# Two residuals moved down ScalarE's queue in an S5 and sparse-MLP kernel

## The chip, the cores and the metric

The kernel runs on one core of a Trainium2 chip. The metric is device time in microseconds (us), best read as the median of several executions. Each execution also has a span, which is the time from the core's first to its last instruction; it is 1.8 to 2.4 us shorter than the time (runs of before).

## The reference, cut to what matters

The input is 2048 tokens of 1024 values, and a core handles them in 16 chunks of 128 tokens.

```python
xn = _layernorm(x)
# A: diagonal state space model, a scan over all tokens
Bu = einsum("bld,pd->blp", xn, B_bar)
h  = Lam_bar * h + Bu[:, t]            # for each token t
yA = 2 * einsum("blp,dp->bld", hseq, Cmat).real + xn * Dskip
# B: the two tokens with the largest xn @ w_r go through a gated MLP;
#    its result is added to xn at those tokens
return x + yA + B(xn)
```

Each chunk thus needs the residual `x + xn`, which is `x * (1 + rstd) - mean * rstd`. This is ScalarE's `xa` (chunks 9 to 12 get theirs from VectorE), and it is added to the matmul result `pY` at the very end of the chunk's work. Chunks go in pairs: chunks 2f and 2f+1 share the matmuls into `pB` and the casts that empty it into `u` (`u` f/j is the j-th of the pair's eight). Other names in the traces: `sum`, `sq`, `rstd` and the negated mean `nmean` are the steps to a chunk's norm `xn`; `xnT` is its transpose, made by a DMA; `gb` is the cast of the scan's result `gf`, and `hT` is made from it for the output matmuls `pY`.

## The kernel before: the parts concerned

The program doesn't write its instructions in a fixed order. A planner in it simulates the engines at build time and emits one operation after another; the smaller `key` goes first among those that are ready. A table `ADJUST` shifts single keys. The emitted order is fixed: on the chip each engine works through its own queue.

```python
ADJUST = {
    ('x', 4): -5.4, ('x', 6): 45.2, ...
    ('Bh', 1, 0): -4.0,
}
...
def add(self, name, eng, dur, fn, deps=(), key=0.0, takes=(), mb=0.0, lag=0.0):
    key += self.adjust.get(name[0], 0.0) + self.adjust.get(name, 0.0)
...
def load_x(c):                      # x for the norm: four buffers
    xt_tiles[c] = xin.tile([128, D], BF16, name="xt")
    nc.sync.dma_start(out=xt_tiles[c][:], in_=x2[c * T:(c + 1) * T, :])
...
def ln_apply_act(c):                # the norm, on ScalarE for chunks 6 to 15 (L375)
    nc.scalar.activation(out=xn_tiles[c][:], in_=xt_tiles.pop(c)[:], func=ACT.Identity,
                         bias=nmr_all[:, c:c + 1], scale=rstd_all[:, c:c + 1])
...
def evac_u(f, j):                   # empties one of the three pB buffers (L653)
    nc.scalar.copy(out=u_tiles[f][:, :, j, :], in_=pB_tiles.pop((f, j))[:])
...
def load_xr(c):                     # x again, for the residual: ONE buffer (L807)
    xr = xrp.tile([128, D], BF16, name="xr")
    nc.sync.dma_start(out=xr[:], in_=x2[c * 128:(c + 1) * 128, :])
    y_tiles["xr", c] = xr

def residual(c):                    # L812
    xa = outp.tile([128, D], F32, name="xa", tag="xa", bufs=1)
    nc.scalar.activation(out=xa[:], in_=y_tiles.pop(("xr", c))[:], func=ACT.Identity,
                         bias=nmr_all[:, c:c + 1], scale=rstd1_all[:, c:c + 1])
...
add(("xa", c), "ACT", 1.13, lambda c=c: residual(c), [("xr", c), ("nmr", c), ("nmr1", c)],
    key=c - 25, takes=xa_take)
```

`xr` has one buffer, so chunk 4's reload can only be issued when residual 3 has been taken, and everything behind residual 4 on ScalarE waits when that reload is late.

## Time and profile before

| | before |
|---|---|
| time, first three runs | 266.67, 265.92, 267.57 us |
| profiled run | 267.47 us, span 265.2 us |
| busy in the span | TensorE 97%, VectorE 95%, ScalarE 60% |
| TensorE's waits from 60 us on | 1.4 us on a `u` cast, 0.4 us in the tail |
| ScalarE's idle time before residual 4 | 1.43 us |

In the profile PE is TensorE, DVE is VectorE, ACT is ScalarE, SPq is SyncE's queue, which issues most DMA transfers. L812 is line 812 of the program. A line of waits reads: engine, line, what it waited for, total us, times, longest. A line of a timeline reads: start, duration, engine, line, operation, output<-inputs, shapes, count, and in brackets the idle time before it and what ended it. The prediction below shows the lines on which it rests.

### The profile page before, as it was taken

The page shows a single profiled execution, that of the slowest core. Times are in us where ns is not written, and L with a number is a line of the kernel's source. Part 1 is how long each engine was busy: PE and PEld are TensorE (multiplying, and loading weights), DVE is VectorE, ACT ScalarE, POOL GpSimd, SP SyncE. Part 2 cuts the span into 40 slices and gives each one's busy share as a digit, 9 for nine tenths or more (in the row PEclk, how much of TensorE's full clock was granted, in tenths as well). Part 3 has the DMA queues.
Part 4 walks back from the last instruction along what each step waited for, and adds up shares of the span by engine and source line. Part 5 has one row for each costly group of instructions (what it writes and reads, how often), then busy time and mean ns, then how long its engine had stood idle before and what let it go on. Part 6 is the DMA issues. An engine that isn't in the chain of part 4 may idle for free.

```text
span 265.2 us, 5503 instructions
## 1 busy us (share of the span) xinstructions
PE 257.2 (97%) x2211; PEld 172.2 (65%) x2211; DVE 250.7 (95%) x329; ACT 159.1 (60%) x281; POOL 82.8 (31%) x126
## 2 busy tenths in 40 slices
PE   6999999999999999979999999999999999999994
PEld 6899888774688557445756586465763776644461
DVE  6999999999999999998979999999998999999992
ACT  3799999968799999796524347124551533145110
POOL 4220304473636430540140226205260409011020
PEclk9999999999999999999999999999999999999999
DMA  8999999996451127416212197588868884780311
GB/s 192 206 213 198 177 282 195 270 280 219 121 158 43 40 59 218 84 40 160 81 59 62 29 360 231 184 274 281 292 229 265 275 299 161 254 303 20 116 47 40
DMA packets 66165, 46.51 MB, mean 175 GB/s; under 512 B 45844, under 2 KB 52122, under 8 KB 66140
## 3 DMA queue, kind: packets, MB, share of 16 engines
q1 hardware_dynamic: 65788, 45.82, 62.9%
q8 instruction: 17, 0.28, 0.5%
q0 software_dynamic: 144, 0.27, 0.4%
q10 hardware_dynamic: 208, 0.07, 0.1%
q14 instruction: 8, 0.07, 0.1%
HBM read 30.94 MB, written 4.20 MB: 133 GB/s over the span
## 4 chain that ended last, share of the span: by engine, by line
PE 54%; DVE 27%; ACT 11%; issue 4%; DMA 3%; DVEq 0%; ACTq 0%
PE pB L647 26%; PE pY L851 22%; DVE gf L720 5%; PE pG L1045 3%; ACT xn L350 2%; DMA xr<-in_A_x_dram 2%; DVE ot L865 2%; DVE gb L713 2%; ACT xa L812 2%; DVE hT L761 2%; ACT xn L344 2%; DVE m L762 2%; DVE st L335 2%; ACT xn L375 1%; DVE v L699 1%
## 5 line engine op out<-in xcount | busy, mean ns | idle before, releaser
L851 PE MATMUL pY<-CT,hT 128*128 128x512 bf16 (+1 forms) x528 | 118.4, 373 | 0.4 <-DVE hT L763 0.4
L647 PE MATMUL pB<-xnT,BT 128*128 128x256 bf16 (+1 forms) x1088 | 117.3, 266 | 1.4 <-ACT u L653 1.4
L647 PEld LDWEIGHTS <-BT 128*128 128x128 bf16 x1088 | 99.4, 98 | 16.5 <-issue 4.7
L851 PEld LDWEIGHTS <-hT 128*128 128x128 bf16 x528 | 49.2, 98 | 52.6 <-issue 3.2
L736 POOL TENSOR_TENSOR cw<-gf,tL 128x16 f32<-128x16 f32 (+1 forms) x38 | 35.1, 926 | 138.3 <-DVE gf L720 137.4
L720 DVE TENSOR_TENSOR_SCAN gf<-R,v 128x1040 f32<-128x1040 f32 (+1 forms) x38 | 69.0, 1851 | 0.2
L653 ACT CAST u<-pB 128x512 bf16<-128x512 f32 x64 | 36.5, 580 | 34.7 <-PE pB L647 34.6
L726 ACT CAST gb<-gf 128x1024 bf16<-128x1024 f32 (+1 forms) x38 | 32.4, 863 | 22.9 <-DVE gf L720 22.8
L812 ACT ACTIVATE xa<-xr,nmr_all,rstd_all 128x1024 f32<-128x1024 bf16 x12 | 14.9, 1241 | 24.3 <-DMA xr<-in_A_x_dram 7.4
L761 DVE TENSOR_TENSOR hT<-gb,E2c 128x2048 bf16<-128x2048 bf16 (+2 forms) x22 | 20.4, 928 | 1.6 <-ACT gb L726 1.6
L701 DVE TENSOR_TENSOR v<-v,m 128x2048 bf16<-128x2048 bf16 (+2 forms) x22 | 20.6, 938 | 0.8
L763 DVE TENSOR_TENSOR hT<-hT,m 128x2048 bf16<-128x2048 bf16 (+2 forms) x22 | 20.5, 934 | 0.8
L699 DVE TENSOR_TENSOR v<-u,E1c 128x2048 bf16<-128x2048 bf16 (+2 forms) x22 | 20.4, 929 | 0.2
L700 DVE TENSOR_TENSOR m<-u,E1s 128x2048 bf16<-128x2048 bf16 (+2 forms) x22 | 20.5, 930 | 0.0
L762 DVE TENSOR_TENSOR m<-gb,E2s 128x2048 bf16<-128x2048 bf16 (+2 forms) x22 | 20.5, 930 | 0.0
L865 DVE TENSOR_TENSOR ot<-pY,xa 128x512 bf16<-128x512 f32 (+1 forms) x25 | 16.0, 656 | 3.1 <-PE pY L854 1.8
L751 POOL CAST v<-cy 128x16 bf16<-128x16 f32 (+1 forms) x19 | 14.1, 744 | 1.4
L350 ACT ACTIVATE xn<-xt,nmean_all 128x1024 bf16<-128x1024 bf16 x12 | 13.8, 1151 | 0.3
L744 POOL TENSOR_TENSOR cy<-cw 128x16 f32<-128x16 f32 (+1 forms) x19 | 12.8, 675 | 1.5
L344 ACT ACTIVATE xn<-xt 128x1024 bf16<-128x1024 bf16 x12 | 12.7, 1055 | 0.0
L375 ACT ACTIVATE xn<-xt,nmr_all,rstd_all 128x1024 bf16<-128x1024 bf16 x10 | 12.4, 1242 | 0.3
L752 POOL TENSOR_TENSOR v<-cy,v 128x16 bf16<-128x16 f32 (+1 forms) x19 | 10.3, 544 | 1.5
(148 smaller groups left out, 184.2 us busy)
## 6 DMA issues: line engine op xcount, KB each, us to landing
wt<-in_B_w_up_dram SPq DMA_DIRECT2D x14, 512.0 KB, 5.0
wt<-in_B_w_gate_dram SPq DMA_DIRECT2D x14, 512.0 KB, 4.3
wt<-in_B_w_down_dram SPq DMA_DIRECT2D x14, 512.0 KB, 3.7
xt<-in_A_x_dram SPq DMA_DIRECT2D x16, 256.0 KB, 3.4
xr<-in_A_x_dram SPq DMA_DIRECT2D x16, 256.0 KB, 2.5
out_dram<-ot SPq DMA_DIRECT2D x31, 128.0 KB, 2.2
Drow<-in_A_Dskip_dram SPq DMA_DIRECT2D x1, 256.0 KB
xnT<-xn SPq DMA_TRANSPOSE x10, 2.8
```

Of the source, the lines that this page charges most:

```text
L647: nc.tensor.matmul(out=pB[:, ri, ts_], lhsT=BT[ri][j][:, k, :], rhs=xnT_tiles[f][:, k, ts_], start=(k == 0), stop=(k == DT - 1))
L653: nc.scalar.copy(out=u_tiles[f][:, :, j, :], in_=pB_tiles.pop((f, j))[:])
L699: nc.vector.tensor_tensor(out=rot, in0=u, in1=both(E1c, js), op=ALU.mult)
L700: nc.vector.tensor_tensor(out=m[:, :, js, :], in0=u[:, ::-1], in1=E1s[:, :, js, :], op=ALU.mult)
L701: nc.vector.tensor_add(out=rot, in0=rot, in1=m[:, :, js, :])
L720: nc.vector.tensor_tensor_scan(out=flat(gf), data0=flat(R[:, js, :]), data1=flat(v[:, ri, js, :]), initial=0.0, op0=ALU.mult, op1=ALU.add)
L726: nc.scalar.copy(out=gb_tiles[c][:, ri, js, :], in_=gf_tiles[c, js.start, ri][:, :, 2:])
L736: nc.gpsimd.tensor_tensor(out=cw_tiles[c, js.start][:, ri, :, 0:n], in0=g.unsqueeze(1).to_broadcast([128, 2, n]), in1=tL[:, ri, :, js], op ...
L761: nc.vector.tensor_tensor(out=rot, in0=g, in1=E2c[:, :, js, :], op=ALU.mult)
L762: nc.vector.tensor_tensor(out=m[:, :, js, :], in0=g[:, ::-1], in1=both(E2s, js), op=ALU.mult)
L851: nc.tensor.matmul(out=pY[:], lhsT=h_tiles[c][:, ri, j, :], rhs=CT[ri][h][:, j, d0:d0 + w], start=first and c in SKIP_DVE and ri == rs[0] ...
L865: nc.vector.tensor_add(out=y_tiles["ot", c][:, d_], in0=y_tiles.pop(("pY", c, dh))[:], in1=y_tiles["xa", c][:, d_])
```

## The change

Its intent is to let ScalarE do urgent things first: residual 4 isn't needed until chunk 4's output is added, and it goes behind the norm of chunk 11; residual 6 goes back by one operation.

```diff
     ('gT', 1): 64.4,
     ('Bh', 1, 0): -4.0,
+    ('xa', 4): 35.0, ('xa', 6): 20.0,
 }
```

No instruction is added or taken away. On ScalarE residual 4 goes behind norm 11; residual 6 goes behind `u` 4/4. The added line shifts line numbers by one, so L812 is L813 in the changed kernel.

## The prediction

> **What bounds the kernel now.** The page's first part and its two waits tables for TensorE and VectorE come first.
>
> ```profile
> PE 257.2 (97%) x2211; PEld 172.2 (65%) x2211; DVE 250.7 (95%) x329; ACT 159.1 (60%) x281; POOL 82.8 (31%) x126
> ```
>
> TensorE and VectorE are both nearly full, ScalarE is at 60%. A change on ScalarE can therefore only pay where ScalarE holds one of the two full engines up. The waits of TensorE from 60 us to the end are just these:
>
> ```profile
> PE pB L647 <- ACT u L653: 1.4, 1, 1.4
> PE pY L851 <- DVE hT L763: 0.4, 1, 0.4
> ```
>
> There is a single wait of 1.4 us on ScalarE (a `u` cast that empties a `pB` buffer), and a 0.4 us one in the tail at 259 us. The chain of work that ended last, around the first, reads (start, duration, what):
>
> ```profile
> 101.57 1.14 ACT xa L812
> 102.71 0.03 ACT lv L314
> 102.73 5.39 DMA xr<-in_A_x_dram
> ...
> 108.20 1.25 ACT xa L812
> 109.45 0.09 ACT nmean_all L382
> 109.54 0.94 ACT gb L726
> ...
> 113.69 0.57 ACT u L653
> 114.27 0.04 issue
> 114.31 1.91 PE pB L647 x16
> ```
>
> So the end of the kernel hangs, at 102.7 us, on a reload of x into `xr`; then ScalarE runs without a gap from the residual (L812) to the `u` cast; then TensorE starts. After 114.31 the chain is TensorE without a wait to 231 us and mostly VectorE after that. The timeline of ScalarE gives the stretch in single operations:
>
> ```profile
> 106.59 0.19 ACT L344 ACTIVATION_READ_ACCUMULATOR xn<-xt 128x1 f32 x1
> 108.20 1.25 ACT L812 ACTIVATE xa<-xr,nmr_all,rstd_all 128x1024 f32<-128x1024 bf16 x1 [1.43 <-DMA xr<-in_A_x_dram]
> 109.36 0.19 ACT L382 ACTIVATE nmean_all<-sm 128x1 f32<-128x1 f32 x1
> 109.44 1.03 ACT L726 CAST gb<-gf 128x1024 bf16<-128x1024 f32 x1
> ...
> 112.55 1.24 ACT L375 ACTIVATE xn<-xt,nmr_all,rstd_all 128x1024 bf16<-128x1024 bf16 x1
> 113.69 0.56 ACT L653 CAST u<-pB 128x512 bf16<-128x512 f32 x1
> ```
>
> The trace shows no chunk numbers. I took them from the order in which the unchanged program's own planner emits ScalarE's work: sum 11, residual 4, negated mean 11, `gb` 5, square 11, rstd 11, norm 11, `u` 4/0, sum 10 and so on. The L812 at 108.20 is thus the residual of chunk 4, and the L375 at 112.55 the norm of chunk 11. VectorE suffers twice nearby, each time on a `gb` cast from ScalarE:
>
> ```profile
> 110.51 1.23 DVE L761 TENSOR_TENSOR hT<-gb,E2c 128x2048 bf16<-128x2048 bf16 x1 [0.42 <-ACT gb L726]
> ...
> 118.50 1.26 DVE L865 TENSOR_TENSOR ot<-pY,xa 128x512 bf16<-128x512 f32 x2
> 120.91 1.23 DVE L761 TENSOR_TENSOR hT<-gb,E2c 128x2048 bf16<-128x2048 bf16 x1 [1.15 <-ACT gb L726]
> ```
>
> The reader should see that the residual isn't urgent (its taker, the L865 of chunk 4, runs at 118.50, nine microseconds after it), and that it stands ahead of things that are.
>
> **What the Trainium skill says.** "PSUM — Partial Sum Buffer", section "Engine vs sequencer instructions": the queues of ScalarE, VectorE and GpSimd are strict FIFO, and matmuls complete in program order. The trace agrees: ScalarE idled 1.43 us before the residual, although the next operation needed only the sum that had ended at 106.78, and `gb` only a scan that VectorE had finished at 106.41. "ScalarE: Activation LUTs", section "What ACT_TABLE_LOAD costs": 186 ns, plus about 93 ns for each per-partition pointer operand, plus 0.833 ns an element, and neighbours overlap by about 93 ns. For 1024 elements with two pointers that is an estimate of 1225 ns; the trace has 1.24 us, and the next operation starts 1.14 to 1.16 us after the residual does. I use the trace's 1.15.
>
> **The change part by part.** Nothing is added or removed: same instructions, another order.
>
> First, residual 4. Without it, the negated mean follows the accumulator read at about 106.81 (0.03 us after its end, as elsewhere in this timeline) instead of 109.36. From there to the `u` cast ScalarE takes 113.69 - 109.36 = 4.33 us, with all its inputs there. So the place behind norm 11 is reached at 106.81 + 4.33 = 111.14. I read "behind the norm" as right behind it, ahead of `u` 4/0. The residual runs there with its data long landed (108.1), and `u` starts at 111.14 + 1.15 = 112.29 instead of 113.69: 1.40 us sooner. That is just the vanished idle time; the residual's own 1.15 us stays ahead of the `u` cast.
>
> TensorE: its matmul before the wait ends at 112.89, the wait is 1.42. The cast would now end at 112.29 + 0.56 = 112.85, so TensorE goes on at about 112.9. **Gain there: 1.4 us.** VectorE: `gb` comes 2.5 us sooner, so the 0.42 wait goes; the second `gb` (119.83, in ScalarE's unbroken run behind `u`) also comes 1.4 sooner, so most of the 1.15 wait goes too: 0.42 + about 1.0 = 1.4 us, no more and no less than TensorE's.
>
> A part may be lost at once. The `pY` ring has three buffers, so chunk 5's second output half (TensorE L844 at 119.93) needs the first L865 of chunk 4. That one ended at 118.50 + 0.68 = 119.18 and moves by only 0.42, to 118.76; TensorE would be there at 119.93 - 1.42 = 118.51. An estimated wait of 0.3 us, giving a net gain of 1.1 to 1.4.
>
> Second, residual 6. It runs at 127.10 after a wait of 3.26 us, and `u` 4/4 stands behind it, starting at 128.25. Letting that cast go first frees a `pB` buffer some 3 us sooner. But the trace shows no TensorE wait there: three `pB` buffers are in turn, and the taker of this one is the third of three matmul groups that start at 128.22 and take 1.75 us each, near 131.7. The taker of the residual itself comes at 135.40, after a wait on TensorE. **Worth 0**, perhaps a guard against a wait that residual 4's shift would have opened.
>
> Sum: 0 for the second, 1.1 to 1.4 us for the first. TensorE has no wait from 114 to 259 us, and what feeds it later (scans, casts, weight loads released by its own matmuls) starts from events that move along. I pass 1.2 us on to the end: 266.7 - 1.2 = 265.5 us, or 0.45%.
>
> **The rivals.** (a) The gain is eaten later: VectorE, at 95%, may hold the old pace. For it: in 150 to 250 us VectorE is idle less than 2 us. Against: its two waits at 110 and 120 go as well, and at 135.40 it waits 1.27 us for TensorE, so it is not the leader there. This would leave 266.2 to 266.7. (b) The late residual becomes a new wait: it frees the only `xr` buffer 2.8 us later (end about 112.3 instead of 109.4), so chunk 5's reload starts later. "DMA: Bandwidth & Descriptors", section "Anatomy of one DMA — SWDGE (gpsimd) path", says a semaphore wait sits on the issuing sequencer, before dispatch. If that reload stayed ahead of norm 11's transpose on SyncE, the transpose (now due 111.2 instead of 113.81) would wait to 112.3, still earlier than before. An unloaded `xr` takes 2.5 us to land here, so by 115 to 116; residual 5 needs it at about 119.4 (120.78 less 1.4). Its single `xa` buffer is free after the two L865 of chunk 4, at 119.76 less 0.42 = 119.34: in time by nothing, so some tenths may go astray. That would make 265.8 to 266.3. (c) More than the sum: if `u` 4/0 were put ahead of the residual, ScalarE would gain 2.5 us on it, but TensorE had only 1.42 to lose, and the rest would be VectorE's; 265.2 at best, not the 261.3 that 2% asks for.
>
> **Range and chances.** The three runs of before spread from 265.92 to 267.57, so a median may be off by about 0.5 us. With that on both sides of 265.5, and rival (a) on the upper side: 264.4 to 266.9. Two per cent is 5.3 us, and the waits that the change can touch sum to 1.4 us on TensorE. Slower by 2% needs a new wait of over 6 us, of which I found none. Faster 0.01, same 0.98, slower 0.01.
>
> **What would show it.** Right: the L812 of chunk 4 starts near 111.1 with no idle time before it; TensorE's 1.4 us wait on `u` is gone or under 0.3; VectorE's waits of 0.42 and 1.15 on `gb` shrink to some tenths together; a small TensorE wait on L865 may stand near 118.5; residual 6 has a `u` cast ahead of it and nothing else differs there; the span falls by about 1.2. Wrong: a new DMA wait of `xr` before residual 5, a transpose that starts later than 113.8, or TensorE waits after 120 us that give the gain back. The likeliest cause of a miss is that the planner also reorders DMA starts or another engine's work, which the change's title doesn't tell.

## The result, and the profile after

| | before | after |
|---|---|---|
| median, 6 runs each | 266.55 us | 266.14 us |
| lowest to highest | 265.92 to 267.57 us | 265.91 to 266.31 us |
| ratio of the fast runs | | 0.998, 95% interval 0.996 to 1.0001 |
| profiled span | 265.2 us | 264.0 us |

A ratio in this document is the mean time of one kernel's fast runs over that of the other's of the same rounds, so it isn't quite the ratio of the medians quoted. The result is "same" at 2%. The interval just includes 1, so these six runs alone don't show a gain clear of noise; all jobs together do (see "Why the prediction was right or wrong"). The two profiles differ by 1.2 us, just what was predicted; the medians differ by 0.41 us, a third of it. And the lowest run is the same for both: what the change took away is the long runs.

The timeline of ScalarE in the changed kernel, to set against the one in the prediction:

```profile
106.58 0.19 ACT L345 ACTIVATION_READ_ACCUMULATOR xn<-xt 128x1 f32 x1
106.80 0.20 ACT L383 ACTIVATE nmean_all<-sm 128x1 f32<-128x1 f32 x1
106.91 1.03 ACT L727 CAST gb<-gf 128x1024 bf16<-128x1024 f32 x1
...
110.00 1.24 ACT L376 ACTIVATE xn<-xt,nmr_all,rstd_all 128x1024 bf16<-128x1024 bf16 x1
111.15 0.56 ACT L654 CAST u<-pB 128x512 bf16<-128x512 f32 x1
111.62 1.24 ACT L813 ACTIVATE xa<-xr,nmr_all,rstd_all 128x1024 f32<-128x1024 bf16 x1
```

No idle time stands in brackets any more: the negated mean (L383) follows the accumulator read at once, the `u` cast starts 2.5 us sooner than before (113.69), and the residual finds its data there. TensorE's waits from 60 us on in the changed kernel:

```profile
PE pY L852 <- issue: 0.5, 3, 0.2
PE pY L852 <- DVE hT L764: 0.4, 1, 0.4
PE pY L845 <- DVE ot L866: 0.2, 1, 0.2
```

The 1.4 us on `u` is gone; a new one of 0.2 us on VectorE's L866 stands in its place. (The 0.5 us of "issue" is in profiles of the kernel before too, e1 for one.) VectorE's timeline has the two places where it waited for a `gb` cast:

```profile
110.00 1.22 DVE L762 TENSOR_TENSOR hT<-gb,E2c 128x2048 bf16<-128x2048 bf16 x1
...
119.48 1.23 DVE L762 TENSOR_TENSOR hT<-gb,E2c 128x2048 bf16<-128x2048 bf16 x1 [0.21 <-ACT gb L727]
```

Of 0.42 and 1.15 us only 0.21 is left; a new wait of 0.32 us on TensorE's `pR` has come in at 124.70. So the mechanism works in the profile as the sum had it. The question for the experiments is where two thirds of the gain went in the median.

### The profile page after: what moved, and what is told of

Read it like the earlier page. It is cut to its first block, busy times and chain, and to the rows that moved or that the text cites. A ratio compares the mean times of both kernels' runs of the same rounds, so it can differ in the third digit from the quotient of the medians.

```text
span 264.0 us, 5484 instructions
## 1 busy us (share of the span) xinstructions
PE 256.6 (97%) x2191; PEld 172.9 (66%) x2211; DVE 250.6 (95%) x329; ACT 159.1 (60%) x281; POOL 83.5 (32%) x126
## 4 chain that ended last, share of the span: by engine, by line
PE 52%; DVE 36%; DMA 3%; issue 3%; ACT 2%; SPq 2%; DVEq 0%
PE pB L648 26%; PE pY L852 20%; DVE gf L721 9%; DVE ot L866 3%; PE pG L1046 3%; DVE hT L762 3%; DVE m L763 3%; DMA CT<-in_A_C_im_dram 2%; DVE v L702 2%; DVE v L700 2%; DVE m L701 2%; SPq L288 2%; DVE gb L714 2%; DVE st L336 2%; DMA xt<-in_A_x_dram 1%
## 5 line engine op out<-in xcount | busy, mean ns | idle before, releaser
L852 PE MATMUL pY<-CT,hT 128*128 128x512 bf16 (+1 forms) x508 | 114.8, 372 | 1.7 <-issue 0.5
L813 ACT ACTIVATE xa<-xr,nmr_all,rstd_all 128x1024 f32<-128x1024 bf16 x12 | 14.9, 1238 | 20.2 <-DMA xr<-in_A_x_dram 6.0
L866 DVE TENSOR_TENSOR ot<-pY,xa 128x512 bf16<-128x512 f32 (+1 forms) x25 | 16.0, 656 | 3.1 <-PE pY L855 1.8
L753 POOL TENSOR_TENSOR v<-cy,v 128x16 bf16<-128x16 f32 (+1 forms) x19 | 11.1, 585 | 1.5
```

The costliest lines, as they stand in the source:

```text
L852: nc.tensor.matmul(out=pY[:], lhsT=h_tiles[c][:, ri, j, :], rhs=CT[ri][h][:, j, d0:d0 + w], start=first and c in SKIP_DVE and ri == rs[0] ...
L866: nc.vector.tensor_add(out=y_tiles["ot", c][:, d_], in0=y_tiles.pop(("pY", c, dh))[:], in1=y_tiles["xa", c][:, d_])
```

## The experiments

**Theory A**: residual 4's stall isn't the same in each run, because the landing of its `xr` load isn't; the one profiled run had a long one, and a run with no stall has nothing to gain. **Theory B**, the rival: the stall is 1.4 us in each run, and the missing part is lost elsewhere or is noise outside the span. Two further rivals are that residual 6 carries part of the effect, and that the order on ScalarE matters by itself, without the load. Where an edit would move line numbers, it was put on an existing line. All twelve runs gave correct results.

### The kernel before, beside itself

The program is unchanged.

> The kernel before, unchanged, run beside itself. Theory A (the gain is the stall of residual 4 on its xr load, and that stall differs from run to run, so the predicted 1.2 us was the stall of the one profiled run): this profile shows another idle time before the L812 of chunk 4 than 1.43 us, and the runs spread over more than 1 us. Theory B (the stall is the same 1.4 us in each run and the missing 0.8 us was lost elsewhere, or is noise outside the span): idle time again near 1.4 us and span near 265.2 us in each run.

The median was 266.73 us (266.48 to 267.17, 6 runs) against 266.41 us (265.8 to 267.49) of the 11 runs of before in the same job, ratio 1.0011, interval 0.9987 to 1.0035. Its profile has the stall at another size (ScalarE's timeline):

```profile
107.69 1.24 ACT L812 ACTIVATE xa<-xr,nmr_all,rstd_all 128x1024 f32<-128x1024 bf16 x1 [0.85 <-DMA xr<-in_A_x_dram]
```

TensorE's wait on `u` was 0.8 us in this run and its span 264.6 us. The spans of the job's 11 runs of before tell it better: six lie at 264.0 to 264.2 us, five at 265.0 to 265.4 us, none between. (The six own runs are less clean: 264.2, 264.3, 264.6, 265.0, 265.1 and 265.3 us.) The best half of before is already as short as the changed kernel. The spread of the times over the six own runs, 0.7 us, is under the 1 us that A expected; the 11 runs of before show 1.7 us.

### The changed kernel, and each half alone

```diff
-    ('Bh', 1, 0): -4.0,
+    ('Bh', 1, 0): -4.0, ('xa', 4): 35.0, ('xa', 6): 20.0,     # e2
+    ('Bh', 1, 0): -4.0, ('xa', 4): 35.0,                      # e3
+    ('Bh', 1, 0): -4.0, ('xa', 6): 20.0,                      # e4
```

> The changed kernel, with the two numbers put on an existing line so that line numbers stay. Theory A: all runs within about 0.5 us of each other and the span at 264.0 us, since the waiting load is off the path; ratio to before near 0.998. Theory B: the same ratio in each round, near 0.9955 if the gain of the profiles is the real one.

> Residual 4 moved alone. Both theories: the whole gain of the change, within 0.2 us of the changed kernel (span near 264.0 us). A rival in which the residual-6 move carries the gain: no gain here.

> Residual 6 moved alone. Both theories: the time and the spread of the kernel before (ratio 1.000 within 0.2%), with u 4/4 about 2.5 us earlier in the profile and no TensorE wait removed.

| | median, us | spans, us | ratio to before |
|---|---|---|---|
| both (e2) | 266.00 | 263.9 to 264.3 | 0.9984 (0.996 to 1.0009) |
| residual 4 alone (e3) | 265.81 | 263.8 to 264.3 | 0.9975 (0.9952 to 0.9998) |
| residual 6 alone (e4) | 266.72 | 264.6 to 265.7 | 1.0016 (0.9991 to 1.0042) |

Residual 4 carries the whole effect, and both kernels that have it lack the long group of spans. The times of e2 spread over 1.0 us, though, and not the 0.5 us that theory A expected; its spans spread over 0.4 us. Residual 6 alone brings nothing; its `u` 4/4 did start earlier, at 125.36 instead of the 127.79 of e1, and nobody was waiting for it. That all six of its runs fell in the long group may be chance; the interval includes 1, so whether this move costs a little by itself is left open. In its profile the stall before residual 4 was 1.03 us.

### The load made later, in both orders

```diff
-        nc.sync.dma_start(out=xr[:], in_=x2[c * 128:(c + 1) * 128, :])
+        for _ in range(2 if c == 4 else 1): nc.sync.dma_start(out=xr[:], in_=x2[c * 128:(c + 1) * 128, :])
```

> The kernel before with chunk 4's xr load issued twice into the same tile, so that residual 4's data lands later; all else in the same order. Theory A and B: the idle time before residual 4 grows by the extra load (0.7 to 2.9 us, depending on whether the second load waits for the first), TensorE's wait on the u cast grows as much, and the span is 264.0 us plus the wait in each run, so slower than before by 0.7 to 3 us.

> The changed kernel with the same doubled load. Theory A and B: the load has until 111.6 us, so the span stays at 264.0 us; at most 0.5 us more if the second load holds SyncE and with it the transpose of chunk 12. A rival in which the gain comes from the order on ScalarE itself and not from the load: as much slower as the kernel before.

In the old order (e5) the median was 268.79 us, ratio 1.0094 (1.0045 to 1.0143), spans 266.3 to 268.8. In the new order (e6) it was 266.92 us, ratio 1.0007 (0.9968 to 1.0045), spans 264.2 to 265.3. The same delay costs the old order 2.4 us more than the new one (mean spans 267.25 and 264.83 us of four runs each; 1.9 us without e5's run of 268.8 us, the one with a clock of 0.99). TensorE's timeline of e5:

```profile
112.63 0.35 PE L426 MATMUL r_ps<-wr_cm,xnT 128*128 128x1 bf16 x8 [1.72 <-DMA xnT<-xn]
116.41 1.91 PE L647 MATMUL pB<-xnT,BT 128*128 128x256 bf16 x16 [1.68 <-ACT u L653]
```

and of e6:

```profile
112.34 0.35 PE L426 MATMUL r_ps<-wr_cm,xnT 128*128 128x1 bf16 x8 [1.51 <-DMA xnT<-xn]
```

In e6 ScalarE takes residual 4 without a wait:

```profile
111.48 1.24 ACT L812 ACTIVATE xa<-xr,nmr_all,rstd_all 128x1024 f32<-128x1024 bf16 x1
```

The reader should see two waits of TensorE in the first and one in the second. The one that both have is a side effect of the edit, which I had sized too small (at most 0.5 us): the second load writes the same tile and waits on SyncE for the first to land, and the transpose of chunk 12 stands behind it in that queue. The wait on `u` is the theory's, and the new order doesn't have it. ScalarE's idle time before residual 4 was 3.61 us in e5, 2.2 us more than in the first profile. That the wait on `u` would grow as much was a miss: it grew only from 1.42 to 1.68 us, since TensorE had by then stood 1.72 us for the transpose. The old order hands a late load on; the new one hides it.

### The load made earlier, with ScalarE's order untouched

The load of chunk 10's x is needed at 114 us, but stands ahead of chunk 4's `xr` load on SyncE. Here it is issued right behind it.

```diff
-    def load_x(c):
+    def load_x(c, late=False):
+        if c == 10 and not late: return
...
-        nc.sync.dma_start(out=xr[:], in_=x2[c * 128:(c + 1) * 128, :])
+        nc.sync.dma_start(out=xr[:], in_=x2[c * 128:(c + 1) * 128, :]); c == 4 and load_x(10, True)
```

> The kernel before, ScalarE's order untouched, but the load of chunk 10's x (256 KB, needed at 114 us) issued right behind chunk 4's xr load instead of ahead of it. Theory A: the stall is the xr load queued behind two x loads; without one of them it lands at least 0.7 us sooner, the runs with a span of 265.0 and more disappear or drop below 264.5, and the time is that of the changed kernel (ratio near 0.998). If the landing varies for another reason: the same two groups of spans as before.

The median was 265.96 us, ratio 0.9976 (0.995 to 1.0002), and all six spans lie at 263.9 to 264.2 us, while the job's 11 runs of before again reached from 263.8 to 265.1. SyncE's queue in the first profile of before, where the two `xt` are the loads of x for chunks 11 and 10:

```profile
100.16 1.05 SPq L283 DMA_DIRECT2D xt<-in_A_x_dram  x2
101.32 0.36 SPq L869 DMA_DIRECT2D out_dram<-ot  x1
102.73 0.34 SPq L807 DMA_DIRECT2D xr<-in_A_x_dram  x1
```

and in e7:

```profile
100.11 0.57 SPq L283 DMA_DIRECT2D xt<-in_A_x_dram  x1
100.79 0.36 SPq L869 DMA_DIRECT2D out_dram<-ot  x1
102.68 0.34 SPq L807 DMA_DIRECT2D xr<-in_A_x_dram  x1
103.08 0.41 SPq L283 DMA_DIRECT2D xt<-in_A_x_dram  x1
```

ScalarE's timeline of e7, and TensorE's waits from 60 us on:

```profile
106.56 0.19 ACT L344 ACTIVATION_READ_ACCUMULATOR xn<-xt 128x1 f32 x1
106.65 1.24 ACT L812 ACTIVATE xa<-xr,nmr_all,rstd_all 128x1024 f32<-128x1024 bf16 x1
...
112.14 0.56 ACT L653 CAST u<-pB 128x512 bf16<-128x512 f32 x1
```

```profile
PE pY L851 <- DVE hT L763: 0.4, 1, 0.4
PE pY L844 <- DVE ot L865: 0.2, 1, 0.2
```

Residual 4 is in its old place and doesn't wait, and TensorE doesn't wait on `u`. One transfer moved on SyncE's queue does what the change does (mean span 264.0 us for both), so taking the stall away is enough for the gain: the order on ScalarE doesn't pay by itself. Nor is the change's third move needed, chunk 5's `xr` load behind the transpose of chunk 11, which e3 and e8 have too: e7 leaves it out. This also names a part of the cause for the late landing: with one 256 KB load of x less ahead of it, the `xr` load landed 3.89 us after its issue in this profile, instead of 5.39 us. That is just in time (landed at 106.57, used at 106.65); the other five runs have no trace, only the same short spans.

### The place that the prediction had in mind

I had read residual 4 as right behind norm 11, ahead of `u` 4/0. A smaller shift gives that order.

```diff
-    ('Bh', 1, 0): -4.0,
+    ('Bh', 1, 0): -4.0, ('xa', 4): 30.0,
```

> Residual 4 right behind norm 11 and ahead of the cast u 4/0, the order that the prediction had read into the change. By the prediction's sum TensorE still waits 0.0 to 0.1 us only there, and the span is 264.0 to 264.2 us, as the changed kernel. If putting u first was needed for the gain: TensorE's wait on u stays at several tenths.

It gave 265.77 us, ratio 0.9964 (0.9939 to 0.9989), spans 263.8 to 264.0 us. TensorE had no wait on `u`, and ScalarE's timeline had:

```profile
111.22 1.23 ACT L812 ACTIVATE xa<-xr,nmr_all,rstd_all 128x1024 f32<-128x1024 bf16 x1
112.35 0.56 ACT L653 CAST u<-pB 128x512 bf16<-128x512 f32 x1
```

The misread place was harmless: 112.35 is still in time for TensorE. The `u` cast at 111.15 in the changed kernel is early by more than TensorE could use.

### Two more looks at before, and a repeat of the two good orders

> The kernel before, one more profile, to catch a run of the shorter group. Theory A: if this run's span is near 264.0 us, residual 4 shows no idle time before it and TensorE no wait on u; if it is near 265.0 us, an idle time near 1.2 us; between the two it follows the idle time. Theory B: 1.4 us whatever the span.

> The same once more: span minus idle time before residual 4 is again 263.8 us within 0.3, as in the profiles so far (265.2 - 1.43 = 263.8; 264.6 - 0.85 = 263.8).

> The changed kernel again, beside the next: spans 263.9 to 264.3 us, TensorE waits 0.2 us on an L865 near 118.6.

> Residual 4 ahead of u 4/0, residual 6 left where it was. If its small lead of 0.3 us in the earlier job is real, its mean is again 0.2 to 0.4 us under the changed kernel's in the same rounds; if it was chance, they are within 0.15 us.

Neither look caught a run of the short group. The first has:

```profile
108.10 1.24 ACT L812 ACTIVATE xa<-xr,nmr_all,rstd_all 128x1024 f32<-128x1024 bf16 x1 [1.43 <-DMA xr<-in_A_x_dram]
```

and the second:

```profile
108.19 1.24 ACT L812 ACTIVATE xa<-xr,nmr_all,rstd_all 128x1024 f32<-128x1024 bf16 x1 [1.28 <-DMA xr<-in_A_x_dram]
```

They do give two more points for the sum "span minus stall", which is the same in each profile of the old order for chunk 4:

| profile | span, us | idle before residual 4, us | difference, us |
|---|---|---|---|
| before | 265.2 | 1.43 | 263.8 |
| e1 | 264.6 | 0.85 | 263.8 |
| e4 (residual 6 moved) | 264.8 | 1.03 | 263.8 |
| e9 | 265.1 | 1.43 | 263.7 |
| e10 | 265.1 | 1.28 | 263.8 |

So the span follows the stall one to one, and with no stall it would be 263.8 us, plus the 0.2 us that TensorE then waits for L865 (as in e7): 264.0 us, where the short group lies. That the short runs have no stall is read from this and from e7; no profile of before caught such a run.

The kept traces leave a doubt here. Their semaphore records tell when chunk 4's `xr` load landed, in the kernels with the new order too. In all 13 traces where the same loads stand ahead of it as in before, it landed 4.55 to 5.49 us after its issue; about 3.9 us would have been in time (e7). If half of all executions had no stall, 13 late landings out of 13 would be a strange chance. In the ten runs e1 to e8, e11 and e12, as in the result's, the trace is that of the first execution listed. The first listed run of before isn't short in any of the three jobs either (265.0, 264.6 and 264.5 us), while 16 of the 30 later ones have 264.2 us or less. So the load may land later in a first or profiled execution than in most others. No run here tests that.

The repeat gave 266.00 us for the changed kernel (ratio 0.9981, 0.9957 to 1.0005) and 265.93 us for the other order (ratio 0.9981, same interval); their means differ by 0.08 us (266.03 and 265.94), within the 0.15 us that stood for chance. The two orders can't be told apart, so no version was found that beats the changed kernel.

## Why the prediction was right or wrong

The range (264.4 to 266.9 us), the forecast "same" and the path on the chip were right. The size of the gain was too large: 1.2 us forecast, 0.41 us between the medians, and 266.14 us where 265.5 was forecast. Over all jobs the mean span fell from 264.48 us (33 runs of before in three jobs) to 264.00 us (18 runs of the changed kernel), by 0.48 us; with a standard error of about 0.1 us, worked out from these 51 spans, that is clear of noise. That the two profiles differ by just the 1.2 us forecast is in part luck: the profile of before fell on a long run, the same from which the sum was made.

1. *What bounds the kernel.* Right. TensorE's one wait in mid-kernel was handed on to the end; taking it away moved the span of the profile by its size, less the new 0.2 us on L866.
2. *"The place behind norm 11 is reached at 106.81 + 4.33 = 111.14."* Right: 111.15.
3. *"Right behind it, ahead of `u` 4/0."* Wrong about the order, without effect. In e8, which has that order, `u` started at 112.35 instead of the forecast 112.29 and TensorE didn't wait.
4. *VectorE gains 1.4 us.* Right: 1.36 us (0.42 and 0.94 of the 1.15), of which the new wait on `pR` takes back 0.32. *A new TensorE wait of 0.3 us on L865.* It came, with 0.2 us.
5. *Residual 6 is worth 0.* Right (e3 against e2, and e4); `u` 4/4 came 2.4 us sooner in e4 than in e1, not some 3. The guess that it guards against a new wait found no support: e3, without it, is as good.
6. *Rival (b), the later `xr` 5 load.* It didn't come true: issued at 112.89, and residual 5 ran at 119.36 with no wait. The planner did reorder a DMA start, which the prediction had named as the likeliest cause of a miss, but harmlessly: the transpose of chunk 11 was put ahead of this load.
7. *Rival (a), the gain is eaten later by VectorE.* Refuted: between the two profiles the span fell by the full 1.2 us. The measured median, 266.14 us, is near the 266.2 that it would have left, but for the reason under 8.
8. *"I pass 1.2 us on to the end: 266.7 - 1.2 = 265.5 us."* This is the step that failed, and the mis-sized term is the stall of 1.43 us. I took it from one profile as the stall of every run and then took it off a median of three. Of the 33 runs of before, 16 have a span of 264.2 us or less, as the changed kernel has, where the sum above leaves next to no room for a stall; 15 have 264.6 or more; 2 lie between. The mean span lay 0.5 us above the changed kernel's, so the change is worth 0.5 us on average: about 1 us in half of the runs, nothing in the other half. The spans show this split. That the stall is what tells the two halves apart is inferred from the five profiles and e7, with the doubt named above. The prediction had even listed the three runs, 265.92 to 267.57, and had taken their spread for an error of the median, to be put "on both sides". A good part of that spread was the effect itself: the profiled run, at 267.47, was one of the long ones.

What stays open is why the `xr` load lands at different times, and whether it lands in time at all in the short runs of before. Its queue neighbours are part of it (e7), but what differs between two runs of the same program no trace here shows.

## What to carry to other kernels

In a queue that works in order, an operation that isn't urgent and waits for a transfer can go behind those that are urgent and ready; here that cost nothing, and it made the spans steadier (263.9 to 264.3 us instead of 263.8 to 265.4) though it hardly moved the median. Before a wait on a DMA is counted as the gain of every run, hold the profiled run's span against the spans of the plain runs. More profiles alone would have warned only of the size: all five of the old order showed a stall, of 0.85 to 1.43 us. If the plain runs spread as widely as the wait is long, perhaps only a part of them has it. And when the lowest run of both kernels is the same, as here, ask whether the change took away a delay of some runs and not a cost of all.

## What the Trainium skill lacked or had wrong

- "DMA: Bandwidth & Descriptors", section "Anatomy of one DMA — SWDGE (gpsimd) path", fits 2.0 us plus bytes over 436,000 per us for DMAs that GpSimd issues, an estimate of 2.6 us for 256 KB. SyncE issues the `xr` loads, and the trace's median for them is close to it (2.5 us). But the fit has no term for what is ahead: behind two loads of x and a store the same 256 KB took 5.39 us in the first profile, and 3.89 us in e7 with one load less.
- No page that I found says how far a landing differs between runs of one program. Here it bears on the result: the idle time before residual 4 was 0.85 to 1.43 us in five profiles with the old order, and 31 of the 33 spans of before lay in two groups, 263.8 to 264.2 us and 264.6 to 265.4 us.
- "Perfetto Trace Analysis", section "Identifying Dependency Chains", explains how to find what an instruction waits on, and doesn't say that one trace is one draw. The trace of before showed 1.43 us where the mean gain over runs was 0.48 us.
- "DMA: Bandwidth & Descriptors", section "Two DMAs through the same engine are not ordered", tells the author to have the issuing engine wait for the first of two dependent transfers. The two loads into one tile in e5 and e6 have such a wait. The section doesn't say what else it holds up: in e5 SyncE issued the second load at 107.37, 4.74 us after the first and just when that had landed, and TensorE then waited 1.72 us (e5) and 1.51 us (e6) for a transpose behind it.
